# Table load, value maxima and warm-up products moved in the first units of a fused attention and feed-forward kernel

## The chip, the cores and the metric

The kernel runs on one core of one Trainium2 chip. The metric is the device time of one execution in microseconds (us); smaller is better. The kernel before took 964.79 us, the median of three runs from 964.17 to 966.63 us.

## The reference

The inputs are q, k and v with 8 batches, 8 heads, 576 positions and 64 values per head, a matrix `omega` of 128 x 64, and two weight matrices, `w_in` of 512 x 2048 and `w_out` of 2048 x 512. The random features and the linear attention are:

```
q_s, k_s = q * scale, k * scale
phi(x):  h = x . omega - |x|^2 / 2;  h = h - max(h over the 128 features);  exp(h) / sqrt(128)
kv = sum over s of k_p[s, m] v[s, d];   z = sum over s of k_p[s, m]
attn = (q_p . kv) / (q_p . z + 1e-6)
```

The attention output is regrouped to 4608 rows of 512, and the feed-forward part gives `h = x @ w_in`, `g = h * tanh(softplus(h))` and `g @ w_out`. Everything is fp32 in the reference; the weights come to the chip as 64-bit floats, 1 MB for each of the eight blocks into which each matrix is cut.

## The kernel before

**Units.** The attention work is cut into units. A key unit `k{b}_{hp}` handles batch b and a pair of heads: it loads 64 x 1152 keys, multiplies them by omega on TensorE (L372 for the first two batches, in fp32), takes the maximum over the features on VectorE (L379), takes the exponential on ScalarE (L384), multiplies the result by the values (L443) and copies the sums out of PSUM on ScalarE (L449, recorded under the helper's L72). A query unit `q{t}` handles 128 rows and eight heads: product with omega, maximum, exponential, transposition on TensorE (L618), product with the key sums (L629), division (L633 to L647), and for the first two units a last transposition (L656, L657) into `xT0`, the input of the feed-forward part. The first six units, nth 0 to 5, are k0_0, k0_1, k0_2, k0_3, q0 and q1. Chunk 0 of the feed-forward part (L723 with fp32 weights) can begin when q0 and q1 have passed.

**Weights.** Eight `w_task`s turn each 1 MB block from 64-bit to 32-bit floats: one ScalarE instruction (L182), two VectorE instructions (L184, L188) and a maximum on VectorE (L192). For later blocks, parts of this are queued behind q1's division or q1's last copy. `w_scale` (L205) then needs all eight maxima, `pow2` makes a scale from them through GpSimd (L114), and `w_split` makes the fp16 parts that the other chunks use.

**Values.** `v_task(0)` takes the maximum of each of the four value tiles of batch 0 (L280), their maximum (L287), and a scale from it. The product L443 of the first two batches reads the values themselves and needs no scale. The scale of batch 0 is first read by the division of q2 (L645).

**Order of the work.** A generator per task yields between its steps; `step` runs the agenda once per slot. This gives the order in the program, which is a priority. A planner at build time then writes the queue of each engine, in order of priority among what it takes to be ready by then. Each engine works through its queue in order, so an instruction that waits holds up all behind it. `tc.issue_after(ins)` puts an instruction behind `ins` in that queue without a wait for its end. `behind(nth)` does so for the two instructions that `anchors[nth]` holds: a unit's last exponential (ScalarE) and its last maximum (VectorE). `AN`, `AM`, `AP` and `AO` say which unit it is for the weight tasks.

**Transfers.** The list `PREL` issues the first transfers: k0_0 to k0_3, the four value tiles, q0, q1, and w_in's eight blocks. Each key and query unit comes in two halves, the first half from SyncE's queue and the second from ScalarE's (`nc.scalar`), and the value tiles alternate between the two. So ScalarE issues eight transfers: four key halves, two value tiles, two query halves.

**Spins.** `spin` issues matmuls whose result nobody reads. Ten with a constant tile (`idle`, fp16, 512 columns) stand at the start. After the exponentials of the first two units there are two each (L396), with the unit's result as the moving operand, so that they wait for it; after those of the next four units one each.

Of the kernel before, what the change touches and what calls it, by code (L numbers as in the profile page):

```python
# [10 lines left out]
F32 = mybir.dt.float32  # L11
# [3 lines left out]
AF = mybir.ActivationFunctionType  # L15
ALU = mybir.AluOpType
AX = mybir.AxisListType
# [13 lines left out]
def tile_kernel(  # L31
# [10 lines left out]
    nc = tc.nc  # L42
    P = 128
    NT, D, H, _ = qT.shape
# [14 lines left out]
    const = ctx.enter_context(tc.tile_pool(name="const", bufs=1))  # L59
# [26 lines left out]

    lnt = const.tile([P, 1], F32, name="lnt")
    dve.memset(lnt, LNT)


    idle = const.tile([P, 512], F16, name="idle")
# [2 lines left out]
    def spin(n, left, right):  # L94
        pi = ps_o.tile([P, 512], F32, tag="o", name=f"spin{nc.next_id()}")
        for _ in range(n):
            nc.tensor.matmul(out=pi[:, 0:right.shape[1]], lhsT=left, rhs=right, start=True, stop=True)
# [64 lines left out]
        return raw  # L162

    @contextmanager
    def behind(nth):
        with ExitStack() as st:
            for ins in anchors.get(nth, ()):
                st.enter_context(tc.issue_after(ins))
            yield

# [94 lines left out]

    vstate = {}

    def fetch_v(b, hp, dma=nc.sync):
        t = sb.tile([P, 10, D1], F32, tag="vf", name=f"vf{b}_{hp}", bufs=5)
        dma.dma_start(out=t, in_=vL[b, hp])  # L270
        return t

    def v_task(b):
        vt = []
        for hp in range(HP):
            vt.append(loaded.pop(f"v{b}_{hp}", None) or fetch_v(b, hp))
        yield 3 if b else 1
        mx = sb.tile([P, HP], F32, tag="vmx", name=f"vmx{b}", bufs=2)
        for hp in range(HP):
            dve.tensor_reduce(  # L280
                out=mx[:, hp:hp + 1], in_=vt[hp][:, :, 0:D], axis=AX.XY, op=ALU.max,
                apply_absolute_value=True,
            )
            yield 0 if hp % 2 == 0 or b == 0 else 1
        am = sb.tile([P, 1], F32, tag="vam", name=f"vam{b}")
        with tc.high_priority(PRIO):
            dve.tensor_reduce(out=am, in_=mx, axis=AX.X, op=ALU.max)  # L287
            p, s = pow2(am, f"v{b}", TOP)
        vstate[b] = (vt, p, s)
# [22 lines left out]
    def fetch_pair(load, name, tag="af", bufs=2, other=nc.sync):  # L312

        half = load.shape[1] // 2
        f = sb.tile([P, half * load.shape[2]], F32, tag=tag, name=f"f{name}", bufs=bufs)
        for a, q in ((0, nc.sync), (1, other)):
            q.dma_start(
                out=f[a * D:(a + 1) * D].rearrange("d (h b) -> d h b", h=half),
                in_=load[:, a * half:(a + 1) * half],
            )  # L320
        return f
# [10 lines left out]
    def features(load, tiles, name, nth, whole):  # L332

        f = loaded.pop(name, None) or (
            fetch_pair if whole else fetch_tails if name[0] == "k" else fetch
        )(load, name)
        yield gap("load", name)
        if not whole:  # L340
            terms = yield from in_parts(f, name, nth)
        n = sum(len(g) for g in tiles)
        by_act = whole
        e = sb.tile([P, n, M], F32, tag="ae", name=f"e{name}", bufs=2)
        mx = sb.tile([P, n], F32, tag="mx", name=f"mx{name}")
        pps, lo = [], 0
        for g in tiles:
            own, tag = (ps_h, "h") if nth < HP and len(pps) == 2 else (ps_a, "a")
            pp = own.tile([P, 4, M], F32, tag=tag, name=f"p{name}_{lo}")
            pps.append((pp, lo, lo + len(g)))  # L350
            lo += len(g)
            if whole:
                continue
            for i, parts in enumerate(g):
                for rows, o in parts:
                    for j, (left, right) in enumerate(terms):
                        nc.tensor.matmul(  # L357
                            out=pp[rows, i, :], lhsT=left[:, o:o + rows.stop - rows.start],
                            rhs=right, start=j == 0, stop=j == len(terms) - 1,
                        )  # L360
        if whole:

            w = f.shape[1]
            order = [(g, i) for i in range(4) for g in (0, -1)] + [(1, 0)] * (len(tiles) - 2)
            mm = None
            for g, i in order:
                for rows, o in tiles[g][i]:
                    a = slice(o // w * D, (o // w + 1) * D)
                    with ExitStack() as st:
                        if mm is not None:  # L370
                            st.enter_context(tc.issue_after(mm.ins))
                        mm = nc.tensor.matmul(  # L372
                            out=pps[g][0][rows, i, :], lhsT=f[a, o % w:o % w + rows.stop - rows.start],
                            rhs=om_f[a], start=True, stop=True,
                        )
        yield 1
        for pp, lo, hi in pps:
            m = hi - lo
            sub = dve.tensor_reduce(  # L379
                out=mx[:, lo:hi], in_=pp[:, :m, :], axis=AX.X, op=ALU.max, negate=by_act  # L380
            )
            if by_act:
                for i in range(m):
                    last = act.activation(  # L384
                        e[:, lo + i, :], pp[:, i, :], AF.Exp, bias=mx[:, lo + i:lo + i + 1]
                    )
            else:
                sub = dve.tensor_tensor(  # L388
                    out=e[:, lo:hi, :], in0=pp[:, :m, :],
                    in1=mx[:, lo:hi].unsqueeze(2).broadcast_to([P, m, M]), op=ALU.subtract,  # L390
                )
        yield gap("exp", name)
        if not by_act:
            last = act.activation(e, e, AF.Exp, bias=lnt)  # L394
        elif nth < 6:
            spin(2 if nth < 2 else 1, ident, e[:, 0:2, :].rearrange("p n m -> p (n m)"))  # L396
        anchors[nth] = (last.ins, sub.ins)
        return e

# [93 lines left out]
    xT = {}  # L493
# [440 lines left out]
    W_LOAD, W_GAP, PRIO = 1, 1, 400  # L934

    AO = (None,) * 8
    AN = (None,) * 5 + (31,) * 3
    AM = (None,) * 3 + (31,) * 5
    AP = (None,) * 7 + (101,)
# [93 lines left out]
    for what in PREL.split():  # L1033
        i = int(what[1:] or 0)
        if what[0] == "k":
            loaded[f"k0_{i}"] = fetch_pair(kT[0, i], f"k0_{i}", *(("af", 2) if i < 2 else ("g", GB)), nc.scalar)
        elif what[0] == "q":
            loaded[f"q{i}"] = fetch_pair(qT[i], f"q{i}", "xT", 3, nc.scalar)
        elif what[0] == "v":
            for hp in range(HP):  # L1040
                loaded[f"v0_{hp}"] = fetch_v(0, hp, (nc.sync, nc.scalar)[hp % 2])
        else:
            loaded[f"w0_{i}"] = fetch_w(0, i, nc.sync)
    start(v_task(0), V0)
# [90 lines left out]
```

## Time and profile before

| | |
|---|---|
| median of three runs | 964.79 us (964.17 to 966.63) |
| profiled execution, its own time | 959.88 us |
| its span, first to last instruction | 958.1 us |
| mean granted TensorE clock | 0.985 |
| TensorE busy | 933.6 us, 97% of the span |
| VectorE busy | 628.9 us, 66% |
| ScalarE busy | 633.5 us, 66% |
| GpSimd busy | 224.7 us, 23% |

In the profile PE is TensorE's matmuls, PEld its weight loads, DVE VectorE, ACT ScalarE, POOL GpSimd and SP SyncE; a q behind the name (ACTq, SPq) is the engine's issuing side. An fp32 matmul has two records. Rows of a timeline give start, length, engine, line, operation, output<-inputs, shapes and count, and in brackets the idle time before with what ended it. Rows of a table of windows give the stretch, its length, then the busy time and the instructions of PE, PEld, DVE, ACT and POOL, then the granted TensorE clock as a share of full speed, the busy share of the DMA engines and GB/s.

### The profile page before, as it was taken

To read this page: it belongs to the slowest core of one execution; us is meant where nothing else is said; L and a number is where in the kernel's file an instruction comes from. 1 tells how busy PE (TensorE), PEld (TensorE's weight loads), DVE (VectorE), ACT (ScalarE), POOL (GpSimd) and SP (SyncE) were. 2 spreads that over 40 slices of the span, in tenths; PEclk is the share of its full clock that TensorE was granted. 3 is DMA by queue.
4 is the path that set the end of the run, shared out by engine and by line. 5 is a ranking of instruction groups with operands and counts; after the bars stand their busy time and mean duration, and the time that the engine had idled before them with its cause. 6 is when DMAs were issued, how large, how long until landed. Compare 5 with 4: busy or idle time off the path is not lost.

```text
span 958.1 us, 20404 instructions
## 1 busy us (share of the span) xinstructions
PE 933.6 (97%) x8558; PEld 671.4 (70%) x8558; DVE 628.9 (66%) x1080; ACT 633.5 (66%) x818; POOL 224.7 (23%) x141
## 2 busy tenths in 40 slices
PE   8999988999999999999999999999999999999998
PEld 5778864767677777777777777777766777777663
DVE  4799896687766666666465665788889656643330
ACT  4668964686878777778667775779676866332231
POOL 0000016242433322332133333222231332100000
PEclk7899999999999999999999999999999999999999
DMA  9767314531631445223431363323552155644410
GB/s 313 247 206 226 106 34 96 114 71 38 151 81 47 96 86 121 61 59 81 96 68 59 74 121 62 92 81 75 135 121 73 34 101 115 171 117 132 133 56 34
DMA packets 148444, 100.25 MB, mean 105 GB/s; under 512 B 112320, under 2 KB 124736, under 8 KB 148352
## 3 DMA queue, kind: packets, MB, share of 16 engines
q1 hardware_dynamic: 147584, 97.43, 40.2%
q10 hardware_dynamic: 768, 1.52, 0.6%
q8 instruction: 67, 1.10, 0.5%
q14 instruction: 25, 0.20, 0.1%
HBM read 58.95 MB, written 13.63 MB: 76 GB/s over the span
## 4 chain that ended last, share of the span: by engine, by line
PE 78%; DVE 11%; ACT 4%; DMA 3%; issue 3%; POOL 0%; ACTq 0%; POOLq 0%; SPq 0%
PE po L892 31%; PE ph L723 25%; PE p_s L826 3%; PE p_a L826 3%; PE pq L357 2%; PE pn L525 2%; PE po L909 2%; PE pkv L443 2%; PE pk L357 2%; PE pkv L475 2%; DVE g L83 2%; DMA qp<-qn 1%; DVE s L758 1%; PE pk L372 1%; DMA vf<-in_vL_dram 1%
## 5 line engine op out<-in xcount | busy, mean ns | idle before, releaser
L892 PE MATMUL po<-wo,g 128*128 128x512 f16 x1632 | 375.2, 380 | 0.0
L723 PE MATMUL ph<-xT,w 128*128 128x256 f16 (+1 forms) x2816 | 342.5, 278 | 0.3 <-ACT xT L657 0.3
L723 PEld LDWEIGHTS <-w 128*128 128x128 f16 x2688 | 261.3, 98 | 46.8 <-issue 0.3
L892 PEld LDWEIGHTS <-g 128*128 128x128 f16 x1632 | 155.2, 98 | 163.7 <-issue 1.9
L83 DVE SCALAR_TENSOR_TENSOR g<-h,us,g 128x1024 f16<-128x1024 f32 (+3 forms) x92 | 118.5, 1299 | 36.1 <-ACT g L72 35.4
L868 ACT ACTIVATE h<-ph,us 128x512 f32<-128x512 f32 (+3 forms) x152 | 83.3, 573 | 76.1 <-PE ph L723 75.4
L81 POOL TENSOR_TENSOR sq<-fq,sq 64x1024 f16<-64x1024 f32 x31 | 71.4, 2305 | 196.3 <-ACT sq L72 73.2
L81 POOL TENSOR_TENSOR sk<-fk,sk 64x1152 f16<-64x1152 f32 x24 | 59.4, 2477 | 112.3 <-ACT sk L72 87.8
L81 POOL TENSOR_TENSOR xs<-x,xs 128x512 f16<-128x512 f32 (+1 forms) x35 | 45.3, 1294 | 153.6 <-DVE xs L74 66.0
L72 ACT ACTIVATE g<-h,us 128x1024 f16<-128x1024 f32 (+3 forms) x80 | 72.6, 932 | 1.2
L394 ACT ACT_TABLE_LOAD x53 | 68.0, 1283 | 5.3 <-DVE ek L388 4.3
L868 ACT ACT_TABLE_LOAD x55 | 70.6, 1283 | 1.0
L379 DVE TENSOR_REDUCE mxq<-pq 128x4 f32<-128x512 f32 x72 | 46.7, 683 | 31.8 <-PE pq L357 29.3
L81 DVE TENSOR_TENSOR qn<-eq,qn 128x1024 f16<-128x1024 f32 x31 | 41.4, 1336 | 36.4 <-ACT qn L72 36.4
L379 DVE TENSOR_REDUCE mxk<-pk 128x4 f32<-128x512 f32 (+1 forms) x96 | 49.6, 548 | 21.0 <-PE pk L372 11.8
L826 PEld LDWEIGHTS <-w 128*128 128x128 f16 x1008 | 58.4, 98 | 5.9
L868 ACT ACTIVATE h<-h,us 128x1024 f32<-128x1024 f32 (+2 forms) x16 | 14.7, 933 | 61.9 <-DVE h L835 61.9
L72 ACT ACTIVATE o<-po,us 128x512 f32<-128x512 f32 (+1 forms) x38 | 25.8, 680 | 40.5 <-PE po L892 40.5
L81 DVE TENSOR_TENSOR kp<-ek,kp 128x1152 f16<-128x1152 f32 x24 | 36.9, 1540 | 23.8 <-ACT kp L72 23.8
L394 ACT ACTIVATE eq<-eq,lnt 128x1024 f32<-128x1024 f32 x31 | 35.6, 1149 | 21.4 <-DVE eq L388 21.1
L81 POOL TENSOR_TENSOR vb<-vf,vb 128x640 f16<-128x640 f32 x24 | 39.8, 1662 | 42.3 <-DVE vb L74 34.0
L835 DVE TENSOR_TENSOR h<-p_s,h 128x512 f32<-128x512 f32 x30 | 20.2, 689 | 43.2 <-PE p_s L826 43.2
(141 smaller groups left out, 1148.8 us busy)
## 6 DMA issues: line engine op xcount, KB each, us to landing
w<-ds SPq DMA_DIRECT2D x48, 256.0 KB, 3.4
vf<-in_vL_dram SPq DMA_DIRECT2D x30, 325.0 KB, 3.3
out_dram<-o SPq DMA_DIRECT2D x36, 256.0 KB, 2.3
fq<-in_qT_dram SPq DMA_DIRECT2D x31, 256.0 KB, 3.5
fk<-in_kT_dram SPq DMA_DIRECT2D x24, 256.0 KB, 3.6
raw<-in_w_out_dram SPq DMA_DIRECT2D x5, 1024.0 KB, 8.6
wo<-in_w_in_dram SPq DMA_DIRECT2D x4, 1024.0 KB, 10.9
raw<-in_w_in_dram SPq DMA_DIRECT2D x4, 1024.0 KB, 13.6
```

Source lines behind the costliest of these rows:

```text
L72: act.activation(out, in_, AF.Copy, scale=scale)
L81: eng.tensor_tensor(out=out, in0=in_, in1=hi, op=ALU.subtract)
L83: eng.scalar_tensor_tensor(out=out, in0=in_, scalar=scale, in1=hi, op0=ALU.mult, op1=ALU.subtract)
L357: nc.tensor.matmul(out=pp[rows, i, :], lhsT=left[:, o:o + rows.stop - rows.start], rhs=right, start=j == 0, stop=j == len(terms) - 1,)
L379: sub = dve.tensor_reduce(out=mx[:, lo:hi], in_=pp[:, :m, :], axis=AX.X, op=ALU.max, negate=by_act)
L394: last = act.activation(e, e, AF.Exp, bias=lnt)
L443: nc.tensor.matmul(out=pkv[:, j, :], lhsT=e[:, t, :], rhs=vt[hp][:, u, :], start=i == 0, stop=i == 4,)
L723: nc.tensor.matmul(out=ph[:, i, :], lhsT=wi(a, k, f) if c else wi0(k, f), rhs=xT[c][:, y, k, :] if c else xT0()[:, k, :], start=n == 0, st ...
L826: nc.tensor.matmul(out=ph[:, i, :], lhsT=left(gr, op_l, i, a, k), rhs=x_region(c, r)[:, y, k0 + k, :], start=n == 0, stop=n == len(mm) - 1,)
L835: dve.tensor_tensor(out=out, in0=bank, in1=in0, op=ALU.add)
L868: act.activation(h[:, :, lo:hi], ph[:, :, lo:hi], AF.Mish, scale=us[:, 0:1])
L892: nc.tensor.matmul(out=po[i], lhsT=gT[c, gr][:, a, f % FG, i * P:(i + 1) * P], rhs=wo(y, f), start=f == 0 and (a, y) == parts[0], stop=f = ...
```

## The change

There are three edits. A one-column exponential `warm` is issued right after the constant that it reads, and of the start's transfers only the four key halves stay with ScalarE; the value tiles and query halves go to SyncE. The maxima of batch 0's values are started in slot 6, not 1, and each is queued behind the last maximum of unit 3, k0_3 (`AV = 3`, of which `first=1` takes the VectorE instruction); the values are entered into `vstate` ahead of it, so that L443 finds them. The spins behind the exponentials of units 0 and 1 go, and eight of the constant tile are queued behind unit 1's last product with omega.

```diff
     dve.memset(lnt, LNT)
+    warm = const.tile([P, 1], F32, name="warm")
+    act.activation(warm, lnt, AF.Exp)
...
-    def behind(nth):
+    def behind(nth, first=0):
         with ExitStack() as st:
-            for ins in anchors.get(nth, ()):
+            for ins in anchors.get(nth, ())[first:]:
                 st.enter_context(tc.issue_after(ins))
             yield
...
-    def fetch_v(b, hp, dma=nc.sync):
+    def fetch_v(b, hp):
         t = sb.tile([P, 10, D1], F32, tag="vf", name=f"vf{b}_{hp}", bufs=5)
-        dma.dma_start(out=t, in_=vL[b, hp])
+        nc.sync.dma_start(out=t, in_=vL[b, hp])
         return t
...
-        yield 3 if b else 1
+        if b == 0:
+            vstate[0] = (vt, None, None)
+        yield 3 if b else 6
         mx = sb.tile([P, HP], F32, tag="vmx", name=f"vmx{b}", bufs=2)
         for hp in range(HP):
-            dve.tensor_reduce(
-                out=mx[:, hp:hp + 1], in_=vt[hp][:, :, 0:D], axis=AX.XY, op=ALU.max,
-                apply_absolute_value=True,
-            )
+            with behind(AV if b == 0 else None, 1):
+                dve.tensor_reduce(
+                    out=mx[:, hp:hp + 1], in_=vt[hp][:, :, 0:D], axis=AX.XY, op=ALU.max,
+                    apply_absolute_value=True,
+                )
...
+            if nth == 1:
+                with tc.issue_after(mm.ins):
+                    spin(8, idle[:, 0:P], idle)
         yield 1
...
-        elif nth < 6:
-            spin(2 if nth < 2 else 1, ident, e[:, 0:2, :].rearrange("p n m -> p (n m)"))
+        elif 1 < nth < 6:
+            spin(1, ident, e[:, 0:2, :].rearrange("p n m -> p (n m)"))
...
+    AV = 3
...
-            loaded[f"q{i}"] = fetch_pair(qT[i], f"q{i}", "xT", 3, nc.scalar)
+            loaded[f"q{i}"] = fetch_pair(qT[i], f"q{i}", "xT", 3)
         elif what[0] == "v":
             for hp in range(HP):
-                loaded[f"v0_{hp}"] = fetch_v(0, hp, (nc.sync, nc.scalar)[hp % 2])
+                loaded[f"v0_{hp}"] = fetch_v(0, hp)
```

## The prediction

> **What bounds the kernel now.** I read the page first, then the stretch up to the first feed-forward products at 48.53 us, where every edit lies, by windows of 3.41 us, the length in which the recorded clock changes. These are rows of the page and of that table of windows.
>
> ```profile
> PE 933.6 (97%) x8558; PEld 671.4 (70%) x8558; DVE 628.9 (66%) x1080; ACT 633.5 (66%) x818; POOL 224.7 (23%) x141
> ...
> L892 PE MATMUL po<-wo,g 128*128 128x512 f16 x1632 | 375.2, 380 | 0.0
> ```
>
> ```profile
> core 0: us, PE busy (x) PEld busy (x) DVE busy (x) ACT busy (x) POOL busy (x), PEclk, DMA share, GB/s
> ...
> 5.01:8.42 3.41, 3.41 (x43) 2.34 (x41) 0.89 (x2) 0.36 (x1) 0.00 (x0) 1.00 1.02 269
> 8.42:11.83 3.41, 1.73 (x14) 1.63 (x12) 2.17 (x3) 2.32 (x6) 0.00 (x0) 1.00 1.05 361
> 11.83:28.90 17.07, 16.09 (x77) 13.14 (x75) 8.45 (x18) 9.40 (x27) 0.38 (x1) 0.50 1.05 376
> 28.90:32.31 3.41, 3.41 (x29) 2.99 (x28) 3.24 (x6) 2.45 (x11) 0.00 (x0) 1.00 1.05 385
> ...
> 240.53:243.94 3.41, 2.09 (x20) 1.62 (x17) 2.97 (x3) 3.21 (x4) 3.02 (x3) 1.00 1.01 212
> 243.94:247.35 3.41, 2.92 (x35) 1.74 (x36) 2.43 (x4) 1.61 (x2) 1.33 (x1) 1.00 0.85 232
> ```
>
> TensorE is the wall: 97% busy over the span. But for 17.07 us, five windows from 11.83 to 28.90, it had half its clock. The window ahead of them held 1.73 us of matmuls; a later window with 2.09 us was followed by a full clock. So a window falls to half somewhere between 1.73 and 2.09 us of work in the one before.
>
> Now the queues of that time: timelines of VectorE, ScalarE, TensorE and SyncE.
>
> ```profile
> 6.66 0.89 DVE L379 TENSOR_REDUCE mxk<-pk 128x4 f32<-128x512 f32 x2 [3.29 <-PE pk L372]
> 9.03 0.82 DVE L280 TENSOR_REDUCE vmx<-vf 128x1 f32<-128x640 f32 x1 [1.48 <-DMA vf<-in_vL_dram]
> ...
> 12.84 0.82 DVE L280 TENSOR_REDUCE vmx<-vf 128x1 f32<-128x640 f32 x1 [0.82 <-DMA vf<-in_vL_dram]
> 13.58 0.68 DVE L379 TENSOR_REDUCE mxk<-pk 128x4 f32<-128x512 f32 x1
> ...
> 16.06 0.69 DVE L184 TENSOR_SCALAR w<-wo 128x1024 int32<-128x1024 int32 x1 [0.34 <-DMA wo<-in_w_in_dram]
> 20.68 0.69 DVE L379 TENSOR_REDUCE mxk<-pk 128x4 f32<-128x512 f32 x1 [3.93 <-PE pk L372]
> ```
>
> ```profile
> 0.72 2.60 ACTq L317 DMA_DIRECT2D fk<-in_kT_dram  x4
> ...
> 7.56 0.47 ACTq L317 DMA_DIRECT2D fq<-in_qT_dram  x1
> 8.06 1.28 ACT L384 ACT_TABLE_LOAD   x1 [8.06 <-DMA fq<-in_qT_dram]
> 9.36 1.40 ACT L384 ACTIVATE ek<-pk,mxk 128x128 f32<-128x128 f32 x5
> 14.29 3.47 ACT L384 ACTIVATE ek<-pk,mxk 128x128 f32<-128x128 f32 x13 [3.54 <-DVE mxk L379]
> ```
>
> ```profile
> 5.46 2.98 PE L372 MATMUL pk<-om_f,fk 64*128 64x128 f32 x40
> 10.12 1.10 PE L97 MATMUL spin<-ek,ident 128*128 128x256 f32 x4 [1.68 <-ACT ek L384]
> ...
> 14.71 1.97 PE L443 MATMUL pkv<-vf,ek 128*128 128x65 f32 x8 [0.98 <-ACT ek L384]
> ...
> 17.34 2.07 PE L97 MATMUL spin<-ek,ident 128*128 128x256 f32 x4
> ...
> 21.54 4.53 PE L443 MATMUL pkv<-vf,ek 128*128 128x65 f32 x20
> ...
> 29.33 2.44 PE L443 MATMUL pkv<-vf,ek 128*128 128x65 f32 x20
> ```
>
> Unit 0's first two maxima were done by 7.55, but ScalarE was still issuing transfers, each of which waited for an earlier one to land, and loaded its table from 8.06 to 9.34: the first exponential came at 9.36. TensorE, out of work, stood still for 1.68 us, the hole that the table of windows shows. On VectorE unit 0's third maximum stood behind four maxima of values, the last of which waited for its transfer until 12.84; so the exponentials stopped until 14.29, and TensorE again until 14.71.
>
> **The change part by part.** *TensorE's share.* From these rows and the next table:
>
> ```profile
> 16.03:59.80 43.77, 41.54 (x277) 33.44 (x277) 33.04 (x54) 26.39 (x69) 0.00 (x0) 0.85 0.74 253
> ...
> 47.18:59.80 12.62, 11.97 (x78) 9.19 (x77) 12.62 (x16) 5.08 (x13) 0.00 (x0) 1.00 0.55 167
> 59.80:134.20 74.40, 74.13 (x579) 61.49 (x579) 69.74 (x129) 66.92 (x114) 5.49 (x5) 1.00 0.49 149
> 8.45:48.53 40.08, 35.60 (x228) 29.28 (x228) 27.01 (x50) 26.25 (x71) 0.38 (x1) 0.79 0.84 290
> ...
> 48.53:134.20 85.67, 85.00 (x648) 70.08 (x649) 81.01 (x141) 71.09 (x124) 5.49 (x5) 1.00 0.50 154
> ```
>
> From 8.45 (end of unit 1's products) to 48.53 TensorE worked 35.60 us. Of this, 16.09 us were at half clock (the row 11.83 to 28.90), which at full clock is 8.05 us less; the two groups of 20 pkv, 4.53 at half and 2.44 us at full clock, bear out the factor. The removed spins are 1.10 us and, at full clock, 2.07 / 2 = 1.04 us. The eight added ones have the shape of L892's matmuls, 375.2 / 1632 = 0.23 us each: 1.84 us, from 8.45 to 10.29. They need nothing but the constant, so they cover the hole. What remains is 35.60 - 8.05 - 2.14 + 1.84 = 27.25 us: without any idle time the feed-forward products begin at 35.7, not 48.53. TensorE alone allows a gain of 12.8 us. From 48.53 to 134.20 it was busy 85.00 of 85.67 us, so what is gained ahead goes on as a shift if the other engines follow.
>
> *Does the clock hold?* In the window after 8.42, 1.84 us of spins come first. With the table loaded and no values in between, unit 0's nine exponentials, 1.40 / 5 = 0.28 us each, run from about 7.4 to 10 and unit 1's to 12.5. So pkv of unit 0 (20 records, 2.44 us) can follow the spins at once, then pk of unit 2 (half of 2.98, 1.49 us), pkv of unit 1, pk of unit 3: 3.9 us of TensorE per unit against 2.5 us of ScalarE. No window up to about 20 us should have less than 2.5 us of work. I take it that the clock holds.
>
> Against this stands the Trainium skill, "TensorE: Matmul & The Clock Gate", section "Part 1: The HAM clock gate", by which the clock halves after an idle window of about 3.4 us and is full again after one busy window. By that rule a hole of 1.68 us would not cost the clock, and a fall would cost half of 3.4 us, 1.7 us, and not 8.05; the sum would have some 6 us less to gain. Here the clock fell after a window that was half busy and stayed down for 17.07 us, 16.09 of them busy; the measurement decides.
>
> *VectorE's share.* It is the second wall: 81.01 of 85.67 us after 48.53. From the landing of the first weight block (16.03) to the weights' common maximum (59.73) it was idle 43.77 - 33.04 = 10.73 us.
>
> ```profile
> L280 DVE TENSOR_REDUCE vmx<-vf 128x1 f32<-128x640 f32 x4 | 3.2, 817 | 2.9 <-DMA vf<-in_vL_dram 2.9
> ...
> L633 DVE TENSOR_SCALAR rd<-pn 128x4 f32<-128x4 f32 x4 | 0.6, 162 | 2.6 <-PE pn L629 2.6
> ```
>
> ```profile
> 59.73 0.16 DVE L205 TENSOR_REDUCE am_w<-wmax 128x1 f32<-128x8 f32 x1
> ...
> 65.70 0.47 DVE L645 SCALAR_TENSOR_TENSOR x<-pn,s_v,rd 128x256 f32<-128x256 f32 x1
> ```
>
> The value maxima, 4 x 0.82 = 3.3 us, move from before 13.6 to behind unit 3's maxima, into this time. They are ahead of q0's maxima and of weight work, all of which waits for them; nobody waits for their result until q2's division at 65.70. Unit 2's three maxima (1.5 us) leave it, being possible before 16. So VectorE can be earlier at 59.8 by at most 10.73 - 3.3 + 1.5 = 8.9 us. The 2.6 us that the divisions wait for pn I keep, a latency that stays: 6.3 us. After that it was idle 74.40 - 69.74 = 4.66 us, waiting for TensorE; TensorE, which can be up to 12.8 us earlier, will shorten this. I take a quarter, 1.2 us: **7.5 us**, bounds 6.3 - 3.3 = 3 (the value maxima delay everything once more) and 12.8.
>
> *The table and the transfers.* The table load (1.28 us) and one small exponential (bounds 0 and 0.28 us by the row above; I take 0.28) stand ahead of ScalarE's key halves, or behind the first of them, should the planner think that `lnt` is not there yet. In the worse case the first half is issued at about 2.3 us, not 0.72.
>
> ```profile
> L317 ACTq DMA_DIRECT2D fk<-in_kT_dram x4: 556/625/710, 0.7 to 2.7; - x4
> ...
> DMA to landing us min/median/max: 2.8/3.8/7.6
> ```
>
> With 2.8 to 3.8 us to landing it is there at 5.1 to 6.1, where TensorE began at 5.46: a cost of 0 to 0.6 us. The other halves have more room. I take 0.3 us, inside the rounding of 7.5. SyncE takes four more transfers, past which w_in's eight blocks are queued.
>
> ```profile
> 4.19 1.50 SPq L270 DMA_DIRECT2D vf<-in_vL_dram  x2
> 6.79 1.79 SPq L317 DMA_DIRECT2D fq<-in_qT_dram  x2
> 8.62 3.40 SPq L161 DMA_DIRECT2D wo<-in_w_in_dram  x4
> ```
>
> A query half takes 0.47 us to issue; the lengths of these groups include waits. Four of them put w_in's first block 0 to 1.9 us later. The DMA engines were full (shares 1.02 to 1.05 above) and the same bytes stand ahead of the block either way, so I take 0; without that cover the first weight work starts 1.9 us late, out of VectorE's slack. The slot of `v_task` and the entry in `vstate` are order only.
>
> The sum against the profiled execution is 959.88 - 7.5 = 952.4 us. That execution was 4.9 us below the median of the runs; from the median it is 964.79 - 7.5 = **957.3 us**.
>
> **The rivals.** *More, TensorE's bound.* If the planner puts weight maxima behind q1's division, VectorE does not hold x back, and most of 12.8 us comes: 11 us, 953.8. For it: L192 is needed only at 59.8. Against: VectorE is busy 12.62 us without pause behind x already.
>
> *The clock falls anyway,* one or two windows later, since unit 2's pk waits for PSUM that unit 0's exponentials hold, or since the gate asks for more. Then the two holes are filled (1.68 + 0.98) and spins saved (1.10 + 2.07 - 1.84), 4.0 us, less up to 3.3 us for the value maxima: 0.7 to 4.0, in the middle 2.3 us, 962.5. So it would also go by the Trainium skill's rule above, under which the hole isn't what halved the clock.
>
> *Given back, or not done as said:* the planner leaves VectorE's order such that unit 2's maxima still stand behind the weight block of 16.03, or the chain up to 134 does not shift: 0 to 2 us, 964.
>
> *Slower: the keys come late.* The first key half behind the table load lands after 6.8 us. Then TensorE is idle over 1.3 us of the window 5.01 to 8.42, its work falls under 2.09 us, and the half clock begins at 8.42. It costs that idle 1.5 us, half of a further window, 1.7 us, and the eight spins at half speed, 1.84 us more, less the 1.3 us of spins saved: 3.7 us, 968.5. It decides from 4.5 us between issue and landing; the median is 3.8, the longest 7.6. In the Trainium skill, "ScalarE: Activation LUTs", section "What ACT_TABLE_LOAD costs", a switch takes 2.66 us with a drain, which would bring this case nearer by 1.38 us; in the rows above the exponential follows at 9.36 on a load that ends at 9.34, and no drain is seen.
>
> **How the numbers follow.** My forecast 0.55, more 0.17, clock falls anyway 0.13, given back 0.07, keys late 0.08. A measurement of this kernel can tell 0.3%, 2.9 us, from no change: faster is below 961.9. The first two cases and a third of the third give 0.76 faster; the rest of the third and the fourth 0.16 the same; 0.08 slower. The range, 951 to 965, leaves out the keys' case and the far end of the second.
>
> **What would show it.** Right: no half clock before 30 us; table load before 3 us; spins directly behind unit 1's pk; unit 0's nine exponentials in one row by 10.5; x of q1 near 39 and the feed-forward products before 42, not 48.53; the weights' common maximum (59.73) near 53. Wrong: 0.50 in a window between 8 and 30, a hole before unit 0's pk, or value maxima directly ahead of q0's maxima with TensorE idle beside them. The prediction fails if VectorE's queue, not TensorE's clock, set the 48.53.

## The result, and the profile after

The kernel after takes 955.63 us, the median of 22 runs from 953.69 to 956.99; the kernel before, run beside it on the same chips, 960.54 us (22 runs, 953.98 to 966.63). The ratio is 0.9943 with a 95% interval of 0.9927 to 0.9958: faster by 4.9 us. The forecast was 957.3 us from a median of 964.79, a gain of 7.5 us. So the time lies 1.7 us from the forecast, but a third of the gain is missing. The time comes out nearer than the gain because the three runs from which the forecast was made lie at the upper end of the 22. The profiled execution takes 955.38 us (before 959.88).

First the totals from the page of the kernel after.

```profile
PE 929.1 (97%) x8558; PEld 667.8 (70%) x8558; DVE 625.7 (66%) x1080; ACT 636.8 (67%) x821; POOL 220.6 (23%) x141
```

TensorE is still the wall, with 4.5 us less of busy time. The table of windows of the kernel after, with the columns explained ahead of the prediction:

```profile
5.01:8.42 3.41, 3.41 (x35) 2.28 (x34) 0.97 (x3) 0.24 (x1) 0.00 (x0) 1.00 0.97 283
8.42:11.83 3.41, 3.41 (x31) 2.27 (x28) 1.98 (x4) 3.41 (x15) 0.00 (x0) 1.00 1.05 340
...
20.40:23.81 3.41, 3.41 (x43) 2.95 (x42) 3.41 (x7) 2.49 (x7) 0.00 (x0) 1.00 1.05 386
23.81:27.22 3.41, 0.07 (x2) 0.00 (x0) 3.41 (x7) 2.69 (x4) 0.00 (x0) 1.00 1.05 388
27.22:40.87 13.65, 10.08 (x42) 8.85 (x42) 10.26 (x16) 7.05 (x20) 0.62 (x1) 0.50 1.05 342
...
8.52:46.98 38.46, 31.31 (x242) 26.67 (x238) 26.92 (x50) 25.60 (x70) 0.62 (x1) 0.82 0.89 301
16.69:58.09 41.40, 33.77 (x238) 28.88 (x238) 34.66 (x55) 23.63 (x57) 0.62 (x1) 0.84 0.81 276
...
58.09:132.66 74.57, 74.57 (x557) 60.20 (x556) 69.66 (x135) 66.61 (x114) 8.72 (x8) 1.00 0.45 144
```

The windows that held the hole of before are full now. But the window from 23.81 holds 0.07 us of matmuls, and behind it the clock is at half for 13.65 us (before 17.07 us, from 11.83). The half clock has moved, and is not gone. The timelines of ScalarE and TensorE, kernel after:

```profile
1.30 1.28 ACT L90 ACT_TABLE_LOAD   x1 [1.30 <-PEq L1131]
1.36 1.29 ACTq L322 DMA_DIRECT2D fk<-in_kT_dram  x2
...
8.18 4.75 ACT L392 ACTIVATE ek<-pk,mxk 128x128 f32<-128x128 f32 x18 [5.38 <-DVE mxk L387]
```

```profile
5.85 3.39 PE L377 MATMUL pk<-om_f,fk 64*128 64x128 f32 x40
9.17 1.90 PE L99 MATMUL spin<-idle 128*128 128x512 f16 x8
10.91 2.34 PE L451 MATMUL pkv<-vf,ek 128*128 128x65 f32 x20
...
21.82 2.06 PE L377 MATMUL pq<-om_f,fq 64*128 64x128 f32 x32
30.79 1.22 PE L99 MATMUL spin<-eq,ident 128*128 128x256 f32 x2 [6.92 <-ACT eq L392]
...
46.98 0.70 PE L731 MATMUL ph<-xT,w 128*128 128x256 f32 x2
```

Up to the query units' products (pq, 21.82 against 31.70 us before) all went as the change wants it: the table is loaded at 1.30 us, the exponentials of two units run in one row of 18, the eight spins fill the hole. At 23.88 us TensorE is almost 10 us ahead. Then it stands still for 6.92 us, waiting for q0's exponentials, and the feed-forward products begin at 46.98 us: 1.55 us of the lead are left. Who held q0's exponentials stands in the timeline of VectorE, kernel after:

```profile
14.44 1.49 DVE L387 TENSOR_REDUCE mxk<-pk 128x4 f32<-128x512 f32 x3 [4.04 <-issue]
...
22.42 0.69 DVE L387 TENSOR_REDUCE mxk<-pk 128x4 f32<-128x512 f32 x1
23.02 2.99 DVE L285 TENSOR_REDUCE vmx<-vf 128x1 f32<-128x640 f32 x4
25.92 1.22 DVE L190 SCALAR_TENSOR_TENSOR w<-wo,w 128x1024 int32<-128x1024 int32 x1
...
27.12 0.68 DVE L186 TENSOR_SCALAR w<-wo 128x1024 int32<-128x1024 int32 x1
...
28.15 1.21 DVE L194 TENSOR_REDUCE wmax<-w 128x1 f32<-128x1024 f32 x1
...
29.33 0.68 DVE L387 TENSOR_REDUCE mxq<-pq 128x4 f32<-128x512 f32 x1
...
41.82 0.16 DVE L641 TENSOR_SCALAR rd<-pn 128x4 f32<-128x4 f32 x1 [3.96 <-PE pn L637]
...
58.09 0.15 DVE L207 TENSOR_REDUCE am_w<-wmax 128x1 f32<-128x8 f32 x1
```

q0's products are there at 23.88 us, its first maximum comes at 29.33. In between stand the four value maxima, 2.99 us, and three instructions of weight work, 3.1 us. The first row shows where the value maxima came from: VectorE is now idle for 4.04 us ahead of unit 2's maxima, where most of them ran before.

The rest of the gain came later. These are TensorE's waits between 47 and 171 us, first of the kernel before, then of the kernel after:

```profile
PE pn L525 <- DMA qp<-qn: 6.5, 2, 3.5
```

```profile
PE ph L731 <- ACT h L876: 2.7, 1, 2.7
PE pn L533 <- DMA qp<-qn: 2.3, 2, 1.8
```

TensorE waited 6.5 us for the transposing transfers of two query tiles (qp) in the one execution. In the other it waited 2.3 us for them and 2.7 us for `h`, which ScalarE writes. From the first feed-forward product to 171 us it stood still for 7.17 us before and 5.45 us after; two windows of 3.41 us at half clock (from 138.13 and 158.61 us) cost 2.97 us before, one (from 136.45 us) 1.70 us after. Together this is 3.0 us in favour of the kernel after.

### The profile page after: what moved, and what is told of

It is laid out like the page before. It is cut to its first block, busy times and chain, and to the rows that moved or that the text cites. A ratio compares the mean times of both kernels' runs of the same rounds, so it can differ in the third digit from the quotient of the medians.

```text
span 953.6 us, 20400 instructions
## 1 busy us (share of the span) xinstructions
PE 929.1 (97%) x8558; PEld 667.8 (70%) x8558; DVE 625.7 (66%) x1080; ACT 636.8 (67%) x821; POOL 220.6 (23%) x141
## 5 line engine op out<-in xcount | busy, mean ns | idle before, releaser
L81 POOL TENSOR_TENSOR sq<-fq,sq 64x1024 f16<-64x1024 f32 x31 | 69.3, 2238 | 159.1 <-issue 86.8
L387 DVE TENSOR_REDUCE mxk<-pk 128x4 f32<-128x512 f32 (+1 forms) x96 | 49.5, 548 | 17.7 <-PE pk L362 8.3
```

Of the source, the lines that this page charges most:

```text
L81: eng.tensor_tensor(out=out, in0=in_, in1=hi, op=ALU.subtract)
L387: sub = dve.tensor_reduce(out=mx[:, lo:hi], in_=pp[:, :m, :], axis=AX.X, op=ALU.max, negate=by_act)
```

## The experiments

The first theory was the prediction's, amended by the profile: the table edit brings the lead, and the new place of the value maxima loses it at q0, through the half clock that follows the 6.92 us stop. The rivals: the wait on VectorE is the loss in itself, and the clock is off the path; or the spins or the transfers do what is put down to the others. All kernels compute the whole reference. They were timed beside the kernel before, whose medians in the three groups were 959.76, 959.73 and 960.20 us. The first group holds the first four kernels below; the third holds the value edit alone, the two parts of the table edit and the last kernel; the second holds the others. Each group ran on a chip of its own, and the kernel after was in none of them. The ratio behind each time is to the kernel before of the same group, with its 95% interval; it is not the quotient of the two medians and differs from it by up to 0.23%. Where two changed kernels are compared, it is by their medians. Across groups a difference of 2 to 3 us is weak evidence, since the intervals of the ratios mostly touch or overlap there.

**Without the spin edit.** The kernel after, with the old spins behind the exponentials of units 0 and 1 and none behind unit 1's products.

```diff
-            if nth == 1:
-                with tc.issue_after(mm.ins):
-                    spin(8, idle[:, 0:P], idle)
...
-        elif 1 < nth < 6:
-            spin(1, ident, e[:, 0:2, :]...)
+        elif nth < 6:
+            spin(2 if nth < 2 else 1, ident, e[:, 0:2, :]...)
```

> The changed kernel with the spins as they were before (two behind the exponentials of units 0 and 1, none of the constant). Theory: with the table early and the values out of the way the first exponentials come at 8.2, so the old spins start at about 9.2, directly behind unit 1's products, and there is no hole: clock 1.00 until about 27, the time within 1.5 us of the changed kernel. Rival, the constant's products hold the clock: without them a window after 8.4 has under 2 us of work, the clock halves before 16 us, and the time is 3 us or more above the changed kernel.

Measured: 956.69 us (955.75 to 960.16), ratio 0.9974 (0.9954 to 0.9993). The windows of this kernel:

```profile
9.77:23.43 13.66, 13.66 (x131) 11.71 (x132) 7.44 (x13) 9.08 (x31) 0.00 (x0) 1.00 1.04 350
23.43:26.84 3.41, 1.36 (x26) 1.17 (x22) 3.41 (x6) 3.32 (x7) 0.00 (x0) 1.00 1.05 387
26.84:40.49 13.65, 8.78 (x36) 7.85 (x36) 11.56 (x19) 6.12 (x18) 0.61 (x1) 0.50 1.05 344
```

The clock holds through the first units without the constant's spins too, and falls at the same place. With the exponentials early, the new spins have almost nothing to cover; their 1.1 us is inside what these intervals can't tell apart.

**Without the value edit.** The kernel after, with the value maxima where they were.

```diff
-        if b == 0:
-            vstate[0] = (vt, None, None)
-        yield 3 if b else 6
+        yield 3 if b else 1
...
-            with behind(AV if b == 0 else None, 1):
+            with behind(None, 1):
```

> The changed kernel with the value maxima as before (slot 1, not queued behind unit 3). Theory: unit 0's third maximum stands behind the values until about 12.8, TensorE has a hole of 1 to 3 us between 11 and 15, the clock halves once between 12 and 19 for 10 to 17 us, but q0's maxima no longer wait for values; these about cancel: the time is that of the kernel before within 3 us. Rival, each edit is worth its own part: the time is 1 to 3 us above the changed kernel.

Measured: 952.03 us (950.79 to 954.58), 0.9939 (0.9916 to 0.9963). By the medians this is 3.6 us below the kernel after, with six runs; the ratios of the two, 0.9939 and 0.9943, do not tell them apart. In its own group the difference is clear: its slowest run lies below the fastest of the kernel without the spin edit, 955.75 us, which has the value edit. Neither of the two expectations had this. Its timeline of TensorE:

```profile
22.09 2.06 PE L375 MATMUL pq<-om_f,fq 64*128 64x128 f32 x32
26.19 0.70 PE L99 MATMUL spin<-eq,ident 128*128 128x256 f32 x2 [2.04 <-ACT eq L390]
...
40.31 2.86 PE L729 MATMUL ph<-xT,w 128*128 128x256 f32 x12 [0.40 <-ACT xT L663]
```

q0's products are as early as in the kernel after, the stop behind them is 2.04 us instead of 6.92, no window up to 121 us has the half clock, and the feed-forward products begin at 40.31 us. That is the start that the prediction had named as right ("before 42"). The planner now puts the value maxima between the maxima of the keys, and not all ahead of unit 0's third, as in the kernel before. VectorE of this kernel:

```profile
9.49 0.82 DVE L283 TENSOR_REDUCE vmx<-vf 128x1 f32<-128x640 f32 x1 [1.84 <-DMA vf<-in_vL_dram]
10.22 0.68 DVE L385 TENSOR_REDUCE mxk<-pk 128x4 f32<-128x512 f32 x1
```

**Without the table edit.** The kernel after, with the eight transfers on ScalarE and no early exponential.

```diff
-    warm = const.tile([P, 1], F32, name="warm")
-    act.activation(warm, lnt, AF.Exp)
...
-            loaded[f"q{i}"] = fetch_pair(qT[i], f"q{i}", "xT", 3)
+            loaded[f"q{i}"] = fetch_pair(qT[i], f"q{i}", "xT", 3, nc.scalar)
...
-                loaded[f"v0_{hp}"] = fetch_v(0, hp)
+                loaded[f"v0_{hp}"] = fetch_v(0, hp, (nc.sync, nc.scalar)[hp % 2])
```

> The changed kernel without the early table load and with eight transfers on ScalarE as before. Theory: the first exponential comes at 9.4 and not 8.2, the eight products of the constant cover that, the clock holds until about 27, and the wait for q0's maxima swallows the 1.2 us: within 1 us of the changed kernel. Rival: the exponentials, 1.2 us later, are the path to q0 and q1, and the time is 1 to 2 us above the changed kernel.

Measured: 961.19 us (959.62 to 968.67), 1.0036 (1.0015 to 1.0058). Spins and value edit together give nothing, and rather lose; both expectations had a time near that of the kernel after, and missed by more than 3 us. VectorE of this kernel:

```profile
7.39 2.14 DVE L385 TENSOR_REDUCE mxk<-pk 128x4 f32<-128x512 f32 x4
17.73 0.69 DVE L184 TENSOR_SCALAR w<-wo 128x1024 int32<-128x1024 int32 x1 [8.19 <-DMA wo<-in_w_in_dram]
18.33 1.48 DVE L385 TENSOR_REDUCE mxk<-pk 128x4 f32<-128x512 f32 x3
```

The planner puts unit 2's maxima behind the first weight block, which lands at 17.7 us, and VectorE does nothing for 8.19 us, though unit 2's products end at 14.86 us. That it does so because it reckons with late exponentials is likely, and not shown. This is the prediction's rival "given back", but in a kernel that is not the one asked about.

**Value maxima still later.** The kernel after, with the value maxima behind q1's maxima.

```diff
-        yield 3 if b else 6
+        yield 3 if b else 7
...
-    AV = 3
+    AV = 5
```

> The changed kernel with the value maxima queued behind unit 5's last maximum (q1), not unit 3's, and v_task started one slot later. Theory, VectorE's order: in the changed kernel q0's maxima came at 29.33 though q's products were ready at 23.9, behind four value maxima (2.99 us) and weight work; TensorE stood still for 6.92 us and its clock fell from 27.22 to 40.87. With the values out of the way q0's maxima come at 24.5 to 26.5, TensorE's hole shrinks to 1 to 3 us, the clock holds or falls for a shorter time, the feed-forward products begin 3 to 9 us earlier than 46.98, and the time is 2 to 7 us below the changed kernel. Rival, VectorE's sum: the same instructions stand ahead of the weights' common maximum, so it comes within 1.5 us of the changed kernel's 58.09 and the time stays within 1.5 us.

Measured: 956.18 us (954.32 to 958.85), 0.9971 (0.9953 to 0.9988). Windows of this kernel:

```profile
22.61:26.02 3.41, 0.76 (x15) 0.57 (x11) 3.41 (x5) 3.02 (x9) 0.00 (x0) 1.00 1.05 386
26.02:36.26 10.24, 10.24 (x43) 9.22 (x44) 8.20 (x14) 5.65 (x18) 0.61 (x1) 0.50 1.05 362
```

q0's first maximum comes at 23.97 us, but 2.65 us of stop remain, and the clock falls all the same. The feed-forward products begin at 43.19 us, 3.8 us before those of the kernel after, and the end does not show it. The weights' common maximum comes at 55.11 us, 2.98 us before that of the kernel after, so the rival's reason fails too. What was ahead is lost behind this point: between 47 and 171 us TensorE waits 6.5 us for the transposing transfers of two query tiles, as in the kernel before. So an earlier q0 alone isn't enough.

**The stop filled.** The kernel after, with 30 products of the constant behind q1's product with omega. They can run from 23.4 us on and cover the stop.

```diff
-            if nth == 1:
+            if nth in (1, 5):
                 with tc.issue_after(mm.ins):
-                    spin(8, idle[:, 0:P], idle)
+                    spin(8 if nth == 1 else 30, idle[:, 0:P], idle)
```

> The changed kernel with thirty more products of the constant behind unit 5's (q1's) last product with omega, some 6.5 us of TensorE, which fill its hole of 23.9 to 30.8 and alter nothing in the queues of VectorE (up to there), ScalarE and SyncE. Theory, the clock: the wait for q0's maxima stays, but no window is empty, the clock stays 1.00 through 41, unit 3's product with the values takes 2.4 and not 4.4 us, the feed-forward products begin 2.5 to 4.5 us earlier than 46.98, and the time is 2 to 4 us below the changed kernel. Rival, the wait on VectorE is the whole loss: what TensorE saves is waited for again, the products begin less than 1 us earlier and the time is within 1 us.

Measured: 956.14 us (952.67 to 957.32), 0.9940 (0.9917 to 0.9963). Windows of this kernel:

```profile
29.81:33.23 3.42, 2.57 (x23) 2.32 (x21) 3.42 (x7) 3.13 (x9) 0.00 (x0) 1.00 1.05 387
33.23:36.64 3.41, 3.41 (x14) 2.57 (x13) 3.31 (x5) 1.99 (x6) 0.00 (x0) 0.50 1.08 312
```

Of 13.65 us at half clock 3.41 are left, and the mean granted clock over the whole execution rises from 0.988 (median of the runs of the kernel after) to 0.996. The time stays: 956.14 against 955.63. In this kernel q0's first maximum is still at 28.94 us. TensorE's first feed-forward product:

```profile
45.04 1.13 PE L731 MATMUL ph<-xT,w 128*128 128x256 f32 x4
```

That is 1.94 us earlier than in the kernel after, more than the rival had and less than the theory, and by the medians the end does not show it. So with the value maxima behind unit 3, the clock taken back buys no time, and as the whole explanation my clock theory falls here. That VectorE's queue is what sets the time then is what remains; this run alone does not show it.

**The same filling, without the value edit.** As above with ten products, on the kernel without the value edit.

> The changed kernel with the value maxima as before (the run without the third edit, 952.03 us) and ten more products of the constant behind unit 5's last product, for its hole of 24.15 to 26.19. The queues of VectorE, ScalarE and SyncE are those of that run. Theory: whether a hole of 2 us costs the clock depends on how the 3.41 us windows fall on it; filled, it never does: the times lie closer together, the median is 0 to 2 us below 952.03. Rival: that hole never cost anything, and the ten products are in the way: 0 to 1 us above it.

Measured: 949.99 us (948.08 to 953.30), 0.9881 (0.9847 to 0.9914). This is the fastest kernel of the study: by the medians it beats the kernel after by 5.6 us, and its slowest run is below the fastest of the kernel after, 953.69. The feed-forward products begin at 40.27 us. In its own group it stands beside the filled kernel with the value edit: the medians are 6.2 us apart, and only its slowest run lies above the fastest of that kernel, 952.67. Against the same kernel without the ten products (952.03) the 2 us are inside the two intervals.

**One edit alone.** The kernel before with the table edit alone, and with the spin edit alone.

> The kernel before with the table edit alone (early table load, four transfers on ScalarE), spins and value maxima as before. Theory, the table edit is the one that counts: the first exponentials at 7.5, the old spins fill TensorE from about 9, no half clock before 20: 951 to 955 us. Rival, the constant's products hold the clock: it halves before 16, and the time is 956 us or more.

> The kernel before with the spin edit alone. Theory: the hole of 8.45 to 10.12 is filled, but the table (to 9.34) and the values (to 12.84) still hold the exponentials, so TensorE is out of work between 13 and 15, the clock halves at 15 to 19 for 10 to 17 us: 0 to 3 us below the kernel before. Rival, the one hole was all: the clock holds to 24 or longer and the time is 951 to 955 us.

Measured: table edit alone 952.39 us (951.12 to 956.15), 0.9908 (0.9875 to 0.9942); spin edit alone 962.44 us (960.97 to 964.57), 1.0023 (0.9999 to 1.0048). By the medians, one edit of the three is thus worth more than all of them; the intervals of the two ratios, 0.9908 and 0.9943, overlap. That the table edit alone is worth at least as much is what the runs show. With it alone, the first exponential and the first feed-forward product stand here (9.36 and 48.53 us before):

```profile
7.29 1.40 ACT L387 ACTIVATE ek<-pk,mxk 128x128 f32<-128x128 f32 x5 [4.48 <-DVE mxk L382]
```

```profile
43.29 2.86 PE L726 MATMUL ph<-xT,w 128*128 128x256 f32 x12 [0.40 <-ACT xT L660]
```

The spin edit alone was expected at 0 to 3 us below the kernel before and lies 2.7 us above it. The windows of this kernel:

```profile
12.46:15.88 3.42, 0.06 (x1) 0.00 (x0) 3.10 (x6) 0.21 (x1) 0.00 (x0) 1.00 1.03 287
15.88:39.77 23.89, 23.68 (x122) 20.12 (x123) 12.30 (x22) 13.47 (x40) 0.38 (x1) 0.50 1.05 367
```

The spins cover the first hole, but the second, behind the four value maxima, is now in one window, and the half clock lasts 23.89 us with TensorE busy in 23.68 of them.

**The value edit alone.** The kernel before with that edit.

> The kernel before with the value edit alone: the four value maxima behind unit 3's maxima, ScalarE with eight transfers and a late table load, the spins as before. Theory A (value maxima behind the keys' cost what they take from VectorE in its busy stretch, and gain nothing that the table edit does not give): as measured beside the table edit, +3 to +4 us, less what unit 0's third maximum gains by no longer standing behind them (the stop of 3.5 us on ScalarE goes): 957 to 961 us, ratio 0.997 to 1.001. Theory B (my prediction's: the value maxima ahead of unit 0's third maximum are a large part of the lost start): TensorE's second stop ends by 12 us instead of 14.71 us, and half the gain of the whole change or more comes: below 957 us, ratio under 0.996.

Measured: 964.22 us (961.36 to 969.06), 1.0051 (1.0024 to 1.0078), above both theories' ranges. Its ScalarE:

```profile
10.01 4.76 ACT L387 ACTIVATE ek<-pk,mxk 128x128 f32<-128x128 f32 x18
```

The 18 exponentials run in one row, from 10.01 us, so the stop of 3.5 us on ScalarE is gone as the prediction thought; yet the kernel is 4 us slower than before. With all eight combinations, medians in us from the four groups of runs, in which the kernel before has 959.73 to 960.54:

| | value maxima as before | value edit made |
|---|---|---|
| neither table nor spin edit | 960.20 | 964.22 |
| spin edit | 962.44 | 961.19 |
| table edit | 952.39 | 956.69 |
| table and spin edit | 952.03 | 955.63 |

The table edit gains 5.6 to 10.4 us in each of its four pairs. The value edit costs 3.6 to 4.3 us in three of its four, and gains 1.3 us in the one where the spins come without the table. Its price without the other edits, 4.0 us, is measured within one group, with an interval of 0.24 to 0.78%. The spin edit moves the time by +2.2, -0.4, -3.0 and -1.1 us, which these runs do not tell from nothing.

**The two parts of the table edit.** The kernel before with the early exponential alone, and with the transfers to SyncE alone.

> The kernel before with one part of the table edit alone: the one-column exponential at the start, while ScalarE keeps its eight transfers. Measured with both parts (the table edit alone): 952.39 us, 0.9908 of before. Theory A (the eight transfers hold ScalarE, and through the planner's order of VectorE also the third maximum of unit 0): the table load moves to about 1.3 us, but ScalarE issues its last query half at 8.0 us as before, so the first exponential comes at 8.1 us against 9.36 (before) and 7.29 (both parts), the four value maxima still stand ahead of unit 0's third maximum, and TensorE still has a hole of over 2 us ahead of 15 us, so that half clock begins before 16 us: 958 to 961 us, ratio 0.998 to 1.001. Theory B (the load itself was what counted): first exponential by 8.1 us, no half clock before 25 us, and at least two thirds of the gain: below 955 us, ratio under 0.994.

> The kernel before with the other part of the table edit alone: value tiles and query halves to SyncE, no early exponential. Theory A (the transfers count): ScalarE has issued its four transfers by about 3.4 us and loads the table in the pause that follows, since the load itself waits for nothing; first exponential at 7.3 us, the maxima of keys and values alternate as with both parts, and the time is that of both parts within 2 us: 950.5 to 954.5 us, ratio 0.989 to 0.994. Theory B (the load counts): the load waits with the first exponential for its maximum and runs from about 7.3 to 8.6 us; the first exponential at 8.6 us, 1.3 us later than with both parts, and at most a third of the gain is left: 956.5 to 960 us.

Measured: early exponential alone 962.96 us (958.34 to 965.87), 1.0022 (0.9997 to 1.0047); transfers alone 956.63 us (955.35 to 959.26), 0.9961 (0.9941 to 0.9982); both together 952.39 us. ScalarE of the kernel with the early exponential alone, then ScalarE and VectorE of the one with the transfers alone:

```profile
7.51 1.36 ACTq L320 DMA_DIRECT2D fq<-in_qT_dram  x2
8.92 1.40 ACT L387 ACTIVATE ek<-pk,mxk 128x128 f32<-128x128 f32 x5 [6.12 <-DMA fk<-in_kT_dram]
...
15.32 2.43 ACT L387 ACTIVATE ek<-pk,mxk 128x128 f32<-128x128 f32 x9 [2.88 <-DVE mxk L382]
```

```profile
3.36 1.28 ACT L385 ACT_TABLE_LOAD   x1 [3.36 <-issue]
7.61 1.40 ACT L385 ACTIVATE ek<-pk,mxk 128x128 f32<-128x128 f32 x5 [2.96 <-DVE mxk L380]
...
26.66 2.47 DVE L380 TENSOR_REDUCE mxq<-pq 128x4 f32<-128x512 f32 x4
```

Loading the table early is worth nothing while ScalarE still issues to 8.87 us: the first exponential comes at 8.92 us, and the second stop stays (2.88 us, behind a maximum that stands after the last value tile). The time lies above theory A's range. The first feed-forward product of this kernel comes at 46.50 us, 0.5 us before that of the kernel after, and yet its profiled execution takes 962.00 us against 955.38: between 47 and 171 us TensorE waits 7.9 us for the transposing transfers of two query tiles. So the start of these products alone doesn't set the time. With the transfers gone, the load runs at 3.36 us of its own accord, in the pause, and the first exponential comes at 7.61 us. So the transfers are the cause of the early first exponential, as theory A had it; but only 3.6 of the 7.8 us come with them, and the time lies in theory B's range. Where the other half comes from is not shown. In the traces VectorE's order further on differs: q0's maxima start at 26.66 us behind the weight work here, at 25.53 with both parts, and the half clock is 17.07 us long against 6.83. But the profiled execution with both parts, 956.15 us, is the slowest of its six, 1.0 us from the one here, so these two traces can't account for 4.2 us. Why the planner orders these differently once the exponential is there was not tried; what it reckons for the table is a guess.

**The clock and VectorE apart.** The kernel with the value maxima behind q1's maxima, and the stop there filled with 30 products: the edits of two kernels above.

> The kernel after with the value maxima behind q1's maxima, not unit 3's (their measured time: 956.18 us, half clock from 26.02 us), and with 30 products of the constant behind q1's product, which fill TensorE's stop there. Theory A (the value edit's loss of 4 us is the place of 3.0 us of value maxima inside VectorE's busy stretch, wherever in it they stand): the clock holds past 36 us, feed-forward products begin at about 41 us as without the value edit, but the end comes no more than 2 us earlier: 953.5 to 956.5 us, ratio 0.993 to 0.997. Theory B (the loss is the stop of TensorE at 25 to 31 us and the half clock that follows it): with both gone, the time is that of the kernel without the value edit and with filling products, 949.99 us: 949 to 952.5 us, ratio 0.988 to 0.992.

Measured: 953.29 us (950.60 to 954.47), 0.9927 (0.9901 to 0.9954), between the two theories' ranges. The profile has no half clock before 138 us. Against the same place of the maxima without filling (956.18), the clock is worth 2.9 us; against the kernel without the value edit and with filling (949.99), the place of the maxima still costs 3.3 us. VectorE of this kernel:

```profile
13.83 1.49 DVE L387 TENSOR_REDUCE mxk<-pk 128x4 f32<-128x512 f32 x3 [4.04 <-issue]
...
27.74 2.99 DVE L285 TENSOR_REDUCE vmx<-vf 128x1 f32<-128x640 f32 x4
```

Wherever the four maxima stand behind the keys', 2.99 us have left a stretch in which VectorE is idle for 4.04 us and have gone to one in which it is the wall. From the first weight work (16.88 us) to the weights' common maximum (52.75 us) VectorE is idle for only 1.57 us. That maximum comes at 51.50 us in the filled kernel without the value edit, so 1.25 of the 3.3 us are there by then; the rest arises later and was not followed. By the medians both hold here: the place costs about 3 us and the fallen clock about 3 us more. Neither 3 us is sharp, as these kernels ran in three different groups.

## Why the prediction was right or wrong

**Right, by the time; the gain was two thirds of what was said.** Against the profiled execution the sum gave -7.5 us, and 955.38 is -4.5. By medians it is -4.9. That the time came within 1.7 us is partly luck: the median it was counted from was 4.25 us above that of the 22 runs, from which the same sum gives 953.0 us. The gain, too, came from other places than the sum had it: of 6.3 us at the start 1.6 came, and of 1.2 us later 2.9.

**TensorE's share: right.** From 8.52 us to the feed-forward products it worked 31.31 us, 10.08 of them at half clock; at full clock this is 31.31 - 5.04 = 26.27 us. The first 0.72 us of it are still unit 1's products, which end at 9.24 us, so 25.6 us are to be set against 27.25 in the prediction. So the cap of 12.8 us was sound. The best kernel begins these products at 40.27 us and uses 8.3 of it.

**"I take it that the clock holds": wrong beyond the place it was worked out for.** Up to about 20 us every window is full, as worked out. The text asked no further, and 7 us later the clock fell, behind q0. The sign "0.50 in a window between 8 and 30" came at 27.22, and the rival "the clock falls anyway", one or two windows later, came in that form, though four to five windows on (27.22 against 11.83). Its cause was not PSUM or the gate but VectorE.

**VectorE's share: the mis-sized term.** It said 6.3 us earlier at the weights' common maximum; measured 59.73 - 58.09 = 1.6 us. The busy time was right: 33.04 + 3.3 - 1.5 = 34.8 us forecast, 34.66 measured. What failed is the sentence on the 2.6 us of idle time that I kept, "a latency that stays". Idle time is 41.40 - 34.66 = 6.74 us, 3.96 of it in one wait for pn, which TensorE computes at half clock behind q0's late exponentials. Beside it the first weight block came 0.66 us later, inside the 0 to 1.9 us named. I counted the value maxima as 3.3 us of work on VectorE, and named what stands behind them ("ahead of q0's maxima and of weight work, all of which waits for them"), but did not follow that wait to TensorE. The sign "value maxima directly ahead of q0's maxima with TensorE idle beside them" appeared nearly so, with three weight instructions between. The last sentence, that the prediction fails if VectorE's queue sets the start, named the cause.

**"Unit 2's three maxima leave it, being possible before 16": right** (14.44 us). The value maxima, though, had cost VectorE little before: they lay in its idle time. Their move was priced as a cost of 3.3 us set against other gains, and 3.6 to 4.3 us is what three of the four pairs above show. That price was about right, but the edit had nothing to set against it: with the table edit made, only the first of them stands ahead of unit 0's third maximum (10.22 us, and 13.58 before).

**"A quarter, 1.2 us" of later idle time: wrong place.** From 58.09 to 132.66 us are 74.57 us, against 74.40 before. But 4.5 - 1.6 = 2.9 us came after that, where TensorE waited less for the transposing transfers and had one window at half clock instead of two. Which edit did it is not settled: among the single kernels above the waits for these transfers went from 1.2 to 8.7 us, and not by any one edit.

**Table and transfers: right.** The load went behind the first key half's issue, the better of the two cases. The keys' products begin at 5.37 to 5.85 us in the kernels with the early exponential, at 5.39 to 5.77 in those without. "Keys come late" did not happen. Nothing was said of its being the only edit that gains: I had put one gain down to three edits.

**The rule on the clock.** The fall behind a window with 0.07 us of work is what the Trainium skill says in "TensorE: Matmul & The Clock Gate", section "Part 1: The HAM clock gate". Its other half, full clock again after one busy window, the filled kernel shows in the first units (33.23 to 36.64) and the others don't there: with the spin edit alone the half clock lasted 23.89 us, 23.68 of them busy. Later falls mostly end after one window, as from 136.45 us in the kernel after, with 3.41 of 3.41 us busy. What a fall costs was not the same everywhere: filling the stop gained nothing by the medians with the value maxima behind unit 3, and 2.9 us with them behind q1.

## What to carry to other kernels

Before an instruction is moved off a critical place in a queue, look at whether it lies in idle time of its engine there, and what stands behind it where it goes; follow that wait to the engine that is the wall. Take a change of several edits apart: here one of three edits brought at least as much as all, and a gain that looks like three small ones may be one. An earlier start is worth only what the rest of the kernel keeps of it: two kernels here began the feed-forward products before the kernel after (46.50 and 43.19 us) and ended no earlier, with longer waits behind. A half clock can cost nothing while another queue is late, as in the filled kernel with the value maxima behind unit 3.

## What the runs showed of the hardware

- **The fall of the clock does not go by recorded busy time alone.** The clock fell behind windows of 3.41 us with 0.06 to 1.73 us of recorded matmuls, but also behind one with 2.57 us (fp32 matmuls of 65 columns for the most part, in the filled kernel), while a window with 1.88 us in the kernel without the value edit, and the one with 2.09 us in the kernel before, were followed by a full clock; so was one with 1.49 us (695.85 to 699.26 us in the kernel without the spin edit). The bounds 1.73 and 2.09 us of the prediction don't hold for all kinds of work; what the gate counts stays open.
- **Its windows lie differently in each execution.** The first changes of the clock that the profiles show lie at 4.82 to 7.04 us, while the first keys' products start at 5.37 to 5.85 in all of them. (That the window runs freely and is met at another point by each run is also in the section of the Trainium skill named above.) The 21 runs of the kernel before in one group went from 954.57 us, with a mean granted clock of 0.996, to 966.72 us, with 0.980; time and clock go together there (correlation -0.94). The kernel after scatters by 3.3 us.
- **The table load did not wait for what its exponential waits for.** With the transfers alone moved, it ran at 3.36 us, 4.25 us before the first exponential, which waited for its maximum; with the early exponential it ran at 1.30 us, beside the issue of ScalarE's own transfers.
